# Attention, dense FFN and routed experts in one kernel: the join of split weight words, the 1e-9 of the softmax, and the order of the first tiles

## The chip, the cores and the metric

One core of a Trainium2 chip runs the whole program. The metric is the device time of one execution in microseconds; the time before is 1401.77 us, the median of three runs (1400.38 to 1402.29). The engines are called PE (TensorE), DVE (VectorE), ACT (ScalarE), POOL (GpSimd) and SP (SyncE, which issues most DMAs).

## The reference, cut to what matters

```python
# q, k, v: (8, 8, 576, 64) float32
k_p = k.reshape(B, H, Sp, 8, D).mean(axis=3)      # Sp = 72
v_p = v.reshape(B, H, Sp, 8, D).mean(axis=3)
scores = q @ k_p.T / 8;  scores -= scores.max(-1)
attn = exp(scores);  attn = attn / (attn.sum(-1) + 1e-9)
x = (attn @ v_p) as 4608 rows of 512
# dense FFN, w_in (512, 2048), w_out (2048, 512): 64-bit floats in DRAM
h = x @ w_in;  g = h if h >= 1, 0 if h <= -1, else (h + 1)**2 / 4
y = g @ w_out
# routed experts: each row goes to one of 8 experts by argmax(y @ w_gate)
out = softmax_weight * (relu(y @ w1[e]) @ w2[e])
```

The factors 64 and 8 of the means and the scale are folded into later constants.

## The kernel before, in words

The 4608 rows are 36 tiles of 128, in ten blocks of three, four or two tiles. Block 0 has tiles 0 to 2. For each block j the kernel runs 16 steps m: `f1(j, m)` multiplies the block's x by a 128-column piece of `w_in` into PSUM bank 0 or 1 (three products of a high and a low part, 12 matmuls), applies the activation, and `f2(j, m)` multiplies the result by a 128-row piece of `w_out` (nine matmuls in block 0). f1 runs two steps ahead (`AHEAD`). While block j runs, the attention of block j + 1 is done in its gaps: the deque `units` holds its pieces in order, and `slot(j, s)`, called twice a step, issues some. All order is written out by hand; an engine's queue is the order of the calls.

The activation of f1 is a relay. L600 on DVE clamps, L601 on ACT squares, then the closure `larger` issues L605 on DVE (the maximum) and L606 on ACT (the high part), and then the closure `lower` issues L264 on DVE (the low part), which also frees the PSUM bank for f1 two steps on. `larger` and `lower` stand in the deque `later`; `flush()` runs what stood in it when it was called, and what those closures append waits for the next flush. So in the first slot of a step `larger` runs, in the second `lower`.

Attention of a tile t: `u_qt` transposes q (L366, copy L368), `u_sc_all` computes the scores (L312), their maxima (L319) and differences (L321) on DVE, `exps` the exponential on ACT (L326), `rest` the row sums (L376), adds 1e-9 (L378), takes the reciprocal (L379), and lets POOL multiply (L390 or L382). `u_pt` brings the probabilities into transposed form (L412, copy L414; tiles 3 to 6 go through DVE transposes and DRAM instead), `u_pv` multiplies by the pooled values (L425) and writes x as a high part (L431, ACT) and a low part (L432, DVE). Keys are pooled by PE with an identity matrix (`u_kp`, L284), or with `pool_kv` by DVE (L249) or by POOL (L252 to L254), values by `pool_kv`.

The weights of the dense FFN come as 64-bit floats and are converted to 32 bits in block 0 alone: 32 conversions, 16 of `w_in` and 16 of `w_out`, in the order `order`, one for each call of `tick()`. A conversion i has three parts. `convert_a`: ACT copies the upper words, scaled (L527), and makes the sign words (L531). `convert_b` puts two word operations for DVE into the deque `pend`: the first (L539) joins the lowest bits and the sign in the PSUM bank `CV`, the second (L542) joins this with the scaled copy. `convert_c`, two ticks later, rounds to a high part on ACT (L549) and takes the low part on POOL (L264). `mix()` takes one element out of `pend`, the first of a conversion being empty; it is called at many places in the attention code, and `tick` begins with `mix(4)`. In block 0 a slot calls `tick` once while conversions last. The sign words have two buffers (`SGN`), the raw words six (`RB`), `CV` one.

The head, from L1106 on, does the attention of tiles 0 to 2 and the first conversions before f1(0, 0). Six conversions are copied in it (`CAHEAD + 1`), and one more with each of the first two calls of f1.

Of the kernel before, what the change touches and what calls it, by code (L numbers as in the profile page):

```python
# [13 lines left out]
ACTF = mybir.ActivationFunctionType  # L14
ALU = mybir.AluOpType
AX = mybir.AxisListType
# [8 lines left out]
def attention_ffn_routed_experts_kernel(  # L25
# [12 lines left out]
    nc = tc.nc  # L38
# [65 lines left out]
    def at(o, n, p=128):  # L104
        return AT[0:p, o:o + n]
# [1 line left out]
    def fx(o, n):  # L107
        return FX[:, o:o + n]

    KB = [at(576 * i, 4 * SP_).rearrange("p (a c) -> p a c", a=4) for i in range(2)]  # L110
    QB = [at(1152 + 512 * i, 512) for i in range(2)]
    QB2 = at(6336, 512)
    QT = at(2176, 512)
    SC = [at(2688, 576), at(7616, 576)]
    HEAD = blocks[0][1]
    RAW = [at(3264 + 512 * i, 512, SP_) for i in range(3)]
    KP = at(4800, 512, SP_)
    PAIR = [at(3264 + 1024 * i, 1024, SP_) for i in range(2)]
    YF = Y.rearrange("p t d -> p (t d)")
# [1 line left out]
          for a in [YF[:, 0:1024], YF[:, 1024:2048], at(5312, 1024)]  # L121
          + [WG.rearrange("p e d -> p (e d)")[:, 1024 * i:1024 * (i + 1)] for i in range(3)]]
    JK = at(7104, 512)
    PZ = at(1152, 768).rearrange("p (a h j) -> p a h j", a=3, j=32)
    PZ0 = at(6336, 768).rearrange("p (a h j) -> p a h j", a=3, j=32)
    PTB = PT.rearrange("p a (b x) -> p (a b) x", b=2)
    QR = at(5312, 2 * CHUNK * 128).rearrange("p (c u i) -> p c u i", c=4, i=32)
# [105 lines left out]
    def load_q(t):  # L233
        if t >= TURN0:
            return
        for p0, p1, b, s in segs(t):
            nc.sync.dma_start(
                out=qb_of(t)[p0:p1].rearrange("p (h d) -> p h d", h=H),
                in_=q[b, :, s:s + p1 - p0, :].rearrange("h s d -> s h d"))
# [19 lines left out]
    def bank():  # L259
        banks.rotate(-1)  # L260
        return banks[-1]
# [6 lines left out]
    def mix(n=1):  # L268
        for _ in range(min(n, len(pend))):
            pend.popleft()()  # L270
# [3 lines left out]
    def flush():  # L274
        for _ in range(len(later)):
            later.popleft()()

    def u_kp(b, c, raw):
# [6 lines left out]
                                 start=(r == 0), stop=(r == 7))  # L285
        nc.scalar.activation(out=KB[b][:, c], in_=pb[:, 0:SP_], func=ACTF.Copy)

    def u_kt_pair(b, c):

        pb = bank()  # L290
        nc.tensor.transpose(pb[:, 0:SP_], KP[:, c * 128:(c + 1) * 128], ident[0:SP_, 0:SP_])
        nc.scalar.activation(out=KB[b][:, c], in_=pb[:, 0:SP_], func=ACTF.Copy)

# [10 lines left out]
    def u_sc_all(t):  # L304
        pbs = [bank(), bank()]
        for c in range(4):
            for g in range(2):
                toks = slice(64 * g, 64 * g + 64)
                kb = KB[(t * 128 + 64 * g) // S % 2]
                for i in range(2):  # L310
                    rows = slice(64 * i, 64 * i + 64)
                    nc.tensor.matmul(pbs[i][toks, c * SP_:(c + 1) * SP_],  # L312
                                     qt_of(t)[rows, c * 128 + 64 * g:c * 128 + 64 * g + 64],
                                     kb[rows, c], start=True, stop=True)
        sc, sc3, smx = sc_of(t), sc3_of(t), smx3[:, t % 3]
        for i in range(2):
            src = pbs[i][:, 0:4 * SP_].rearrange("p (h c) -> p h c", h=4)
            hs = slice(i, H, 2)
            nc.vector.tensor_reduce(out=smx[:, hs], in_=src, axis=AX.X, op=ALU.max)  # L319
            mix()  # L320
            nc.vector.tensor_tensor(out=sc3[:, hs], in0=src,  # L321
                                    in1=smx[:, hs].to_broadcast([128, 4, SP_]), op=ALU.subtract)
        wide[0] = True

        def exps():
            nc.scalar.activation(out=sc, in_=sc, func=ACTF.Exp, scale=1.0 / 64)  # L326
            finish(t)
        if HEAD <= t < TURN0:
            later.append(exps)
        else:  # L330
            exps()
# [1 line left out]
    smx3 = sb.tile([128, 3, H, 1], F32, name="smx3")  # L333
    ssm3 = sb.tile([128, 3, H, 1], F32, name="ssm3")

    SCH = at(6848, 576)
    PTX = [WOF[2][0:SP_], WOF[3][0:SP_], PT[:, 0], PT[:, 1]]

    def qt_of(t):
        return FR if t == 1 else QT  # L340
# [1 line left out]
    def sc_of(t):  # L342
        return SCH if t == 2 else SC[t % 2]

    def sc3_of(t):
        return sc_of(t).rearrange("p (h c) -> p h c", h=H)

    def pt_of(t, hf):
        return PTX[(2 * t + hf) % 4] if t < HEAD else PT[:, hf]

    def u_qt(t):
        if t >= TURN0:
# [19 lines left out]
    def finish(t):  # L372
        sc3, ssm = sc3_of(t), ssm3[:, t % 3]

        def rest():
            nc.vector.tensor_reduce(out=ssm, in_=sc3, axis=AX.X, op=ALU.add)  # L376
            mix()
            nc.vector.tensor_scalar(ssm, ssm, 1e-9, None, op0=ALU.add)  # L378
            nc.vector.reciprocal(out=ssm, in_=ssm)  # L379
            if turned(t):  # L380
                eng = nc.vector if t >= TURN0 else nc.gpsimd
                eng.tensor_tensor(out=sc3, in0=sc3, op=ALU.mult,  # L382
                                  in1=ssm.to_broadcast([128, H, SP_]))
            elif t >= HEAD:
                later.append(norm)
            else:
                norm()

        def norm():
            nc.gpsimd.tensor_tensor(out=sc3, in0=sc3, in1=ssm.to_broadcast([128, H, SP_]),  # L390
                                    op=ALU.mult)
        later.append(rest)
# [59 lines left out]
    def load_pair(c):  # L452
        for i in range(2):
            load_kv(1, 2 * c + i, PAIR[c % 2][:, 512 * i:512 * (i + 1)])
# [63 lines left out]
    def cvt_dst(i):  # L518
        m, o = order[i]
        return (WOF[m % 4] if o else DFI[m % 3]), RB[i % NRB].rearrange(  # L520
            "p a (x w) -> p a x w", w=2)

    def convert_a(i):
        dst, rb = cvt_dst(i)

        high = rb[:, :, :, 1].bitcast(F32)
        nc.scalar.activation(out=dst.rearrange("p (a x) -> p a x", a=8), in_=high,  # L527
                             func=ACTF.Copy, scale=2.0 ** -112)

        sign = SGN[i % 2].bitcast(F16).rearrange("p (a x w) -> p a x w", a=8, w=2)  # L530
        nc.scalar.activation(out=sign[:, :, :, 1], in_=high, func=ACTF.Copy, scale=2.0 ** -60)  # L531

    def convert_b(i):

        dst, rb = cvt_dst(i)
        di, ci, sg = (x.bitcast(I32).rearrange("p (a x) -> p a x", a=8)
                      for x in (dst, CV, SGN[i % 2]))
        pend.append(lambda: None)
        pend.append(lambda: nc.vector.scalar_tensor_tensor(  # L539
            out=ci, in0=rb[:, :, :, 0], scalar=29, in1=sg, op0=ALU.logical_shift_right,  # L540
            op1=ALU.bitwise_or))
        pend.append(lambda: nc.vector.scalar_tensor_tensor(  # L542
            out=di, in0=di, scalar=3, in1=ci, op0=ALU.logical_shift_left, op1=ALU.bitwise_or))

    def convert_c(i):
        m, o = order[i]
# [25 lines left out]
    def tick():  # L572

        n = ticks[0]
        mix(4)
        if n > 0:
            more_raw(n - 1 + NRB)
        for f, i in ((convert_c, n - 2), (convert_a, n), (convert_b, n)):
            if 0 <= i < len(order) and order[i]:
                f(i)  # L580
        ticks[0] += 1

    def load_out(g):
# [522 lines left out]
    with tc.manual_schedule():  # L1106

        wgp = WG.rearrange("p e d -> p (e d)")[0:SP_]
        raw0 = [WG[0:SP_, i] for i in range(8)] + RAW + [
            FX[0:SP_, 512 * i:512 * (i + 1)] for i in range(1, 5)] + [PT[:, 0]]  # L1110
        hu = [tile_units(t) for t in range(HEAD)]

        def head_pool(i, eng):
            pool_kv(0, i, raw0[i], eng)

        def run_units(n):
            for _ in range(n):
                units.popleft()[1]()
            if qloads:
                qloads.popleft()()  # L1120

        load_q(0)
        for i in range(H):
            load_kv(0, i, raw0[i])
        load_q(1)
        load_q(2)
        for i in range(H, 2 * H):
            load_kv(0, i, raw0[i])
        for i in range(3):
            more_raw(i)  # L1130
        hu[0][0]()
        for c in range(2):
            u_kp(0, c, wgp[:, 1024 * c:1024 * (c + 1)])
        for i in (4, 5):
            head_pool(i, nc.vector)
        for i in (6, 7):
            head_pool(i, nc.gpsimd)
        nc.gpsimd.memset(WG[:, 6:8], 0.0)
        for i in range(3, NRB):
            more_raw(i)  # L1140
        hu[1][0]()
        for c in range(2, 4):
            u_kt_pair(0, c)
        for i in (8, 10, 12):
            head_pool(i, nc.gpsimd)
        hu[0][2]()
        hu[1][2]()
        hu[2][0]()
        head_pool(9, nc.vector)
        head_pool(14, nc.gpsimd)  # L1150
        flush()
        hu[2][2]()
        head_pool(15, nc.gpsimd)
        for i in (11, 13):
            head_pool(i, nc.vector)
        load_pair(0)
        load_pair(1)
        flush()
        tick()
        kv = deque([pair_step(c) for c in range(4)] + [kv_step(1, i) for i in range(H, 2 * H)])  # L1160
        line = [(0, 3), (0, 5), (1, 3), (0, 6), (1, 5), (2, 3), (1, 6), (2, 5), (2, 6)]
        for i, (t, n) in enumerate(line):
            hu[t][n]()
            flush()
            if i in (0, 2, 4, 6):
                tick()
        while ticks[0] < CAHEAD + 1:
            tick()
        banks.clear()
        banks.extend(ps[6:8])  # L1170

# [57 lines left out]
        for m in range(AHEAD):  # L1229
            f1(0, m)  # L1230
            flush()
            tick()
        for g, (j, m) in enumerate(steps):
            if m == 0:
                if j:
# [221 lines left out]
```

## Time and profile before

| what | value |
|---|---|
| median of three runs | 1401.77 us |
| the profiled execution, its own time | 1404.79 us |
| its span, from the first to the last instruction | 1402.8 us |
| busy in the span: PE, DVE, ACT, POOL | 97%, 55%, 31%, 26% |
| mean granted clock of TensorE | 0.993 |

Shares of busy time are means over stages with different limits: in a stretch PE may be full while the others idle, or DVE while PE waits. Durations of instructions that follow each other on one engine overlap a little, so the distance of two starts can be less than the duration of the first. In a timeline an entry in brackets is the idle time before an instruction and what ended it. Block 0 begins with the f1 at 38.11 us.

### The profile page before, as it was taken

How to read it: one execution, taken by the hardware profiler on the slowest of the kernel's cores; microseconds unless marked ns; L12 is line 12 of the kernel's file. 1: busy time of each engine (PE TensorE's matmuls, PEld its weight loads, DVE VectorE, ACT ScalarE, POOL GpSimd, SP SyncE). 2: the span in 40 equal slices, each digit the busy share in tenths (PEclk: the TensorE clock that was granted, in tenths of full speed). 3: DMA queues.
4: the chain of work that ended last, by engine and by line, in shares of the span. 5: the costliest groups of instructions: out<-in, count | busy, mean ns of one | idle time of the engine just before them, and what ended most of it. 6: DMA issues, size and time to landing. Idle time of an engine off the chain costs nothing. (4 is left out here: it accounts for less than half of the span.)

```text
span 1402.8 us, 22101 instructions
## 1 busy us (share of the span) xinstructions
PE 1357.5 (97%) x8082; PEld 1112.8 (79%) x8082; DVE 778.1 (55%) x1577; ACT 433.7 (31%) x729; POOL 358.7 (26%) x520
## 2 busy tenths in 40 slices
PE   6878999999999999999999999999999999999998
PEld 4767778878878778788788888888878888888786
DVE  5798556565666666575666556455532333323426
ACT  4567332222222222223222223343111111111335
POOL 5384736004304203413310011022221211111212
PEclk9999999999999999999999999999999999999999
DMA  9786647436636555545553344572543223331235
GB/s 254 226 261 240 182 136 214 129 122 194 164 124 187 153 149 168 171 155 143 165 157 111 98 152 130 192 263 72 195 129 106 91 74 113 99 111 61 79 127 187
DMA packets 170701, 213.45 MB, mean 152 GB/s; under 512 B 83432, under 2 KB 114440, under 8 KB 170569
## 3 DMA queue, kind: packets, MB, share of 16 engines
q1 hardware_dynamic: 135992, 102.29, 25.2%
q10 hardware_dynamic: 26784, 88.16, 18.8%
q0 software_dynamic: 7792, 21.35, 4.8%
q8 instruction: 69, 1.13, 0.3%
q14 instruction: 64, 0.52, 0.1%
HBM read 188.30 MB, written 47.03 MB: 168 GB/s over the span
## 5 line engine op out<-in xcount | busy, mean ns | idle before, releaser
L593 PE MATMUL ps<-XT,W 128*128 128x512 f32 (+2 forms) x640 | 243.8, 381 | 6.8 <-DVE FG L264 3.0
L595 PE MATMUL ps<-XT,W 128*128 128x512 f32 (+2 forms) x640 | 237.9, 372 | 2.7 <-POOL W L264 2.7
L594 PE MATMUL ps<-XT,W 128*128 128x512 f32 (+2 forms) x640 | 238.1, 372 | 0.2 <-DVE XT L432 0.2
L621 PE MATMUL ps<-WO,FG 128*128 128x512 f32 x576 | 231.6, 402 | 1.3 <-ACT FX L601 1.1
L622 PE MATMUL ps<-WO,FG 128*128 128x512 f32 x576 | 225.9, 392 | 0.0
L623 PE MATMUL ps<-WO,FG 128*128 128x512 f32 x576 | 225.2, 391 | 0.0
L601 ACT ACTIVATE FX<-FX,half 128x512 f32<-128x512 f32 (+2 forms) x152 | 104.0, 684 | 386.0 <-DVE FX L600 348.2
L600 DVE TENSOR_SCALAR FX<-ps 128x512 f32<-128x512 f32 (+2 forms) x152 | 96.7, 636 | 117.7 <-PE ps L595 116.9
L593 PEld LDWEIGHTS ps<-XT,W 128*128 128x128 f32 x640 | 121.8, 190 | 32.1 <-issue 3.4
L719 POOL DMA_INDIRECT perm_d<-idt,POSI x36 | 35.2, 978 | 417.6 <-DVE SM L705 353.0
L993 DVE SCALAR_TENSOR_TENSOR FG<-ps,FG 128x512 fp32r<-128x512 f32 (+1 forms) x64 | 43.2, 675 | 175.4 <-ACT FG L992 172.9
L595 PEld LDWEIGHTS ps<-XT,W 128*128 128x128 f32 x640 | 121.7, 190 | 22.3 <-POOL W L264 4.0
L605 DVE TENSOR_TENSOR ps<-FX,ps 128x512 f32<-128x512 f32 (+2 forms) x152 | 97.5, 641 | 72.8 <-ACT FX L601 71.4
L594 PEld LDWEIGHTS ps<-XT,W 128*128 128x128 f32 x640 | 121.7, 190 | 17.8 <-DVE XT L432 0.5
L621 PEld LDWEIGHTS ps<-WO,FG 128*128 128x128 f32 x576 | 108.5, 188 | 26.4 <-issue 3.0
L623 PEld LDWEIGHTS ps<-WO,FG 128*128 128x128 f32 x576 | 108.6, 188 | 23.7
L606 ACT ACTIVATE FG<-ps 128x512 fp32r<-128x512 f32 (+2 forms) x160 | 88.8, 555 | 123.9 <-DVE ps L605 112.2
L264 DVE TENSOR_TENSOR FG<-ps,FG 128x512 fp32r<-128x512 f32 (+2 forms) x160 | 100.8, 630 | 44.3 <-ACT FG L606 40.6
L622 PEld LDWEIGHTS ps<-WO,FG 128*128 128x128 f32 x576 | 108.7, 189 | 19.8
L252 POOL TENSOR_TENSOR AT<-AT 72x256 f32<-72x256 f32 x106 | 81.2, 766 | 136.3 <-DMA AT<-in_v_dram 68.7
L992 ACT ACTIVATE FG<-ps 128x512 fp32r<-128x512 f32 (+1 forms) x64 | 37.4, 584 | 244.8 <-PE ps L989 231.2
L987 PE MATMUL ps<-XT,W 128*128 128x512 f32 (+1 forms) x256 | 98.9, 386 | 2.9 <-ACT XT L971 2.5
(230 smaller groups left out, 2176.0 us busy)
## 6 DMA issues: line engine op xcount, KB each, us to landing
WO<-wo_d ACTq DMA_DIRECT2D x144, 512.0 KB
AT<-in_moe_w_dram SPq DMA_DIRECT2D x30, 1024.0 KB
p_d<-AT SPq DMA_DIRECT2D x29, 384.0 KB
AT<-in_v_dram SPq DMA_DIRECT2D x59, 144.0 KB
wo_d<-WO SPq DMA_DIRECT2D x16, 512.0 KB
AT<-in_k_dram SPq DMA_DIRECT2D x56, 144.0 KB
PT<-p_d SPq DMA_DIRECT2D x58, 128.0 KB
yrow_d<-Y ACTq DMA_DIRECT2D x7, 1032.0 KB
```

The lines of the kernel that those rows point to most:

```text
L264: eng.tensor_tensor(out=lo, in0=x, in1=r32(hi), op=ALU.subtract)
L593: nc.tensor.matmul(o, wi(m, 0, c), xh, start=(c == 0), stop=False)
L594: nc.tensor.matmul(o, wi(m, 0, c), xl, start=False, stop=False)
L595: nc.tensor.matmul(o, wi(m, 1, c), xh, start=False, stop=(c == KD - 1))
L600: nc.vector.tensor_scalar(r, o, -1.0, 1.0, op0=ALU.max, op1=ALU.min)
L601: nc.scalar.activation(out=r, in_=r, func=ACTF.Square, scale=0.5, bias=half)
L605: nc.vector.tensor_tensor(out=o, in0=r, in1=o, op=ALU.max)
L606: nc.scalar.activation(out=gh, in_=o, func=ACTF.Copy)
L621: nc.tensor.matmul(o, gh, WO[:, g % 4, 0], start=(m == 0), stop=False)
L622: nc.tensor.matmul(o, gh, WO[:, g % 4, 1], start=False, stop=False)
L623: nc.tensor.matmul(o, gl, WO[:, g % 4, 0], start=False, stop=(m == KF - 1))
L987: nc.tensor.matmul(o, e1(0)[:, c, ms], xh, start=(c == 0), stop=False)
```

## The change

- The scaled copy of the upper words (L527) goes into the PSUM bank `CV` and no longer into the target buffer. The first word operation shifts it in place and joins the sign words, the second joins the lowest bits, out of the raw words, and writes the target.
- The copies of a conversion (`convert_ab`) are put into `later` by `tick`, and run in the next flush.
- The scores of a tile have a 73rd column for each head, which is set to 1e-9 once; the row sum takes it in, and L378 falls away. Buffers move to make room.
- In the head, the exponentials of tiles 0 to 2 are called by hand, the memset of the sign words comes first, DVE pools three key heads, POOL one, and four value heads are summed by PE (`u_vp`: eight matmuls of 192 columns and eight of 64); before, `pool_kv` did all eight, three of them on DVE and five on POOL, and now POOL does the other four. Tiles 0, 1 and 2 are finished one after the other; their probabilities have six buffers.
- Four conversions are copied before f1(0, 0) where it was six. Three more ticks follow f1(0, 0), one f1(0, 1).

The diff, cut to what the steps touch (moved buffers mostly left out):

```diff
@@ -285,6 +287,19 @@
+    def u_vp(more):
+        pb = bank()
+        n = len(RAW)
+        raw = at(RAW0, n * 512, SP_).rearrange("p (h r d) -> p h r d", h=n, r=8)
+        for x, h0, h1 in ((raw, 0, n), (more.rearrange("p (h r d) -> p h r d", h=1, r=8), n, n + 1)):
+            dst = pb[0:SP_, h0 * D:h1 * D].rearrange("p (h d) -> p h d", h=h1 - h0)
+            for r in range(8):
+                nc.tensor.matmul(dst, ident[0:SP_, 0:SP_], x[:, :, r], start=(r == 0),
+                                 stop=(r == 7))
+        nc.scalar.activation(out=VS[:, 0, 0:(n + 1) * D], in_=pb[0:SP_, 0:(n + 1) * D],
+                             func=ACTF.Copy)
     def u_kt_pair(b, c):
@@ -323,9 +338,9 @@
         def exps():
-            nc.scalar.activation(out=sc, in_=sc, func=ACTF.Exp, scale=1.0 / 64)
+            nc.scalar.activation(out=sc3, in_=sc3, func=ACTF.Exp, scale=1.0 / 64)
             finish(t)
-        if HEAD <= t < TURN0:
+        if t < TURN0:
             later.append(exps)
@@ -333,8 +348,8 @@
-    SCH = at(6848, 576)
-    PTX = [WOF[2][0:SP_], WOF[3][0:SP_], PT[:, 0], PT[:, 1]]
+    SCH = at(6848, SCW)
+    PTX = [VS[:, 1], FR[0:SP_], PT[:, 0], PT[:, 1], WOF[2][0:SP_], WOF[3][0:SP_]]
@@ -342,11 +357,14 @@
+    def sc4_of(t):
+        return sc_of(t).rearrange("p (h c) -> p h c", h=H)
     def sc3_of(t):
-        return sc_of(t).rearrange("p (h c) -> p h c", h=H)
+        return sc4_of(t)[:, :, 0:SP_]
     def pt_of(t, hf):
-        return PTX[(2 * t + hf) % 4] if t < HEAD else PT[:, hf]
+        return PTX[2 * t + hf] if t < HEAD else PT[:, hf]
@@ -373,9 +391,9 @@
         def rest():
-            nc.vector.tensor_reduce(out=ssm, in_=sc3, axis=AX.X, op=ALU.add)
-            mix()
-            nc.vector.tensor_scalar(ssm, ssm, 1e-9, None, op0=ALU.add)
+            nc.vector.tensor_reduce(out=ssm, in_=sc4_of(t), axis=AX.X, op=ALU.add)
+            if t >= HEAD:
+                mix()
             nc.vector.reciprocal(out=ssm, in_=ssm)
@@ -521,10 +539,10 @@
     def convert_a(i):
-        dst, rb = cvt_dst(i)
+        _, rb = cvt_dst(i)
         high = rb[:, :, :, 1].bitcast(F32)
-        nc.scalar.activation(out=dst.rearrange("p (a x) -> p a x", a=8), in_=high,
+        nc.scalar.activation(out=CV.rearrange("p (a x) -> p a x", a=8), in_=high,
                              func=ACTF.Copy, scale=2.0 ** -112)
@@ -537,10 +555,15 @@
         pend.append(lambda: nc.vector.scalar_tensor_tensor(
-            out=ci, in0=rb[:, :, :, 0], scalar=29, in1=sg, op0=ALU.logical_shift_right,
+            out=ci, in0=ci, scalar=3, in1=sg, op0=ALU.logical_shift_left, op1=ALU.bitwise_or))
+        pend.append(lambda: nc.vector.scalar_tensor_tensor(
+            out=di, in0=rb[:, :, :, 0], scalar=29, in1=ci, op0=ALU.logical_shift_right,
             op1=ALU.bitwise_or))
-        pend.append(lambda: nc.vector.scalar_tensor_tensor(
-            out=di, in0=di, scalar=3, in1=ci, op0=ALU.logical_shift_left, op1=ALU.bitwise_or))
+    def convert_ab(i):
+        mix(len(pend))
+        convert_a(i)
+        convert_b(i)
@@ -575,9 +598,10 @@
             more_raw(n - 1 + NRB)
-        for f, i in ((convert_c, n - 2), (convert_a, n), (convert_b, n)):
-            if 0 <= i < len(order) and order[i]:
-                f(i)
+        if 0 <= n - 2 < len(order) and n != 3:
+            convert_c(n - 2)
+        if n < len(order):
+            later.append(lambda: convert_ab(n))
         ticks[0] += 1
@@ -1106,7 +1130,7 @@
         wgp = WG.rearrange("p e d -> p (e d)")[0:SP_]
-        raw0 = [WG[0:SP_, i] for i in range(8)] + RAW + [
+        raw0 = [WG[0:SP_, i] for i in range(6)] + [VS[:, 1], PT[:, 1]] + RAW + [
             FX[0:SP_, 512 * i:512 * (i + 1)] for i in range(1, 5)] + [PT[:, 0]]
@@ -1119,53 +1143,66 @@
+        nc.gpsimd.memset(WG[:, 6:8], 0.0)
+        for t in range(3):
+            nc.gpsimd.memset(sc4_of(t)[:, :, SP_:SP_ + 1], 1e-9)
         load_q(0)
...
         load_q(2)
-        for i in range(H, 2 * H):
+        for i in (12, 13, 8, 9, 10, 11, 14, 15):
             load_kv(0, i, raw0[i])
...
             u_kp(0, c, wgp[:, 1024 * c:1024 * (c + 1)])
-        for i in (4, 5):
+        for i in (4, 5, 6):
             head_pool(i, nc.vector)
-        for i in (6, 7):
-            head_pool(i, nc.gpsimd)
-        nc.gpsimd.memset(WG[:, 6:8], 0.0)
+        head_pool(7, nc.gpsimd)
         for i in range(3, NRB):
...
             u_kt_pair(0, c)
-        for i in (8, 10, 12):
+        for i in (12, 13, 14):
             head_pool(i, nc.gpsimd)
         hu[0][2]()
+        hu[2][0]()
+        later.popleft()()
         hu[1][2]()
-        hu[2][0]()
-        head_pool(9, nc.vector)
-        head_pool(14, nc.gpsimd)
+        rest = later.popleft()
+        later.popleft()()
+        rest()
+        head_pool(15, nc.gpsimd)
+        later.popleft()()
+        hu[2][2]()
+        exps2 = later.popleft()
+        tick()
         flush()
-        hu[2][2]()
-        head_pool(15, nc.gpsimd)
-        for i in (11, 13):
-            head_pool(i, nc.vector)
+        u_vp(raw0[11])
+        exps2()
         load_pair(0)
         load_pair(1)
+        hu[0][3]()
+        flush()
+        hu[0][5]()
+        hu[0][6]()
+        tick()
+        flush()
+        hu[1][3]()
+        hu[1][5]()
+        hu[1][6]()
+        tick()
+        hu[2][3]()
+        hu[2][5]()
+        convert_c(1)
+        hu[2][6]()
         flush()
         tick()
+        flush()
         kv = deque([pair_step(c) for c in range(4)] + [kv_step(1, i) for i in range(H, 2 * H)])
-        line = [(0, 3), (0, 5), (1, 3), (0, 6), (1, 5), (2, 3), (1, 6), (2, 5), (2, 6)]
-        for i, (t, n) in enumerate(line):
-            hu[t][n]()
-            flush()
-            if i in (0, 2, 4, 6):
-                tick()
-        while ticks[0] < CAHEAD + 1:
-            tick()
         banks.clear()
@@ -1229,7 +1266,9 @@
             flush()
-            tick()
+            while ticks[0] < CAHEAD + 2 + m:
+                tick()
+                flush()
         for g, (j, m) in enumerate(steps):
...
                 if j:
```

## Rows read from the trace of the kernel before

**Rows 1.** Stretches: us, busy PE, PEld, DVE, ACT, POOL (count), granted clock, DMA, GB/s.

```profile
68.00:141.10 73.10, 59.89 (x431) 48.69 (x430) 67.59 (x110) 50.95 (x90) 46.56 (x51) 0.93 0.75 250
...
124.70:141.10 16.40, 15.91 (x106) 13.56 (x107) 13.39 (x26) 10.83 (x19) 8.04 (x9) 0.81 0.44 160
...
200.00:400.00 200.00, 200.00 (x1277) 161.01 (x1274) 126.22 (x253) 57.15 (x93) 52.31 (x97) 1.00 0.55 159
```

**Rows 2.** The same view, of line 539 alone: DVE busy time and instructions.

```profile
68.00:141.10 73.10, 21.11 (x20) 0.93 0.75 250
```

**Rows 3.** The same view, of line 378 alone.

```profile
68.00:141.10 73.10, 4.54 (x4) 0.93 0.75 250
```

**Rows 4.** Timeline of DVE in block 0: start, duration (us), line, shapes.

```profile
42.31 0.56 DVE L600 TENSOR_SCALAR FX<-ps 128x384 f32<-128x384 f32 x1 [1.81 <-PE ps L595]
...
68.06 0.56 DVE L600 TENSOR_SCALAR FX<-ps 128x384 f32<-128x384 f32 x1 [1.72 <-PE ps L595]
...
105.29 1.42 DVE L539 SCALAR_TENSOR_TENSOR ps<-WG 128x512 int32<-128x512 int32 x1
106.82 0.69 DVE L542 SCALAR_TENSOR_TENSOR FX<-FX,ps 128x512 int32<-128x512 int32 x1
...
108.66 0.55 DVE L605 TENSOR_TENSOR ps<-AT,ps 128x384 f32<-128x384 f32 x1
109.12 0.69 DVE L539 SCALAR_TENSOR_TENSOR ps<-WG 128x512 int32<-128x512 int32 x1
109.84 0.69 DVE L542 SCALAR_TENSOR_TENSOR FX<-FX,ps 128x512 int32<-128x512 int32 x1
110.45 0.55 DVE L264 TENSOR_TENSOR FG<-ps,FG 128x384 fp32r<-128x384 f32 x1
110.92 0.55 DVE L600 TENSOR_SCALAR FX<-ps 128x384 f32<-128x384 f32 x1
...
141.07 0.51 DVE L600 TENSOR_SCALAR FX<-ps 128x384 f32<-128x384 f32 x1
```

**Rows 5.** Timeline of ACT beside those.

```profile
109.24 0.49 ACT L606 ACTIVATE FG<-ps 128x384 fp32r<-128x384 f32 x1 [1.23 <-DVE ps L605]
109.63 0.62 ACT L549 ACTIVATE W<-FX 128x512 fp32r<-128x512 f32 x1
110.15 0.67 ACT L527 ACTIVATE FX<-WG 128x512 f32<-128x512 f32 x1
110.71 0.80 ACT L531 ACTIVATE WG<-WG 128x512 f16<-128x512 f32 x1
```

**Rows 6.** Timeline of the head and the first steps, several engines.

```profile
8.13 1.98 DVE L249 TENSOR_REDUCE AT<-WG 72x64 f32<-72x512 f32 x2 [6.89 <-DMA WG<-in_k_dram]
...
12.78 0.95 POOL L1138 MEMSET WG<- 128x1024 f32 x1
...
13.09 1.24 PE L312 MATMUL ps<-AT 64*64 64x72 f32 x32
...
15.22 1.11 PE L366 MATMUL ps<-ident,AT 128*128 128x128 f32 x4
...
21.38 2.77 PE L412 MATMUL ps<-ident,AT 128*72 128x128 f32 x12 [0.99 <-POOL AT L390]
...
27.57 1.12 PE L425 MATMUL ps<-FX,VS 72*64 72x128 f32 x8 [0.53 <-ACT FX L414]
...
38.11 0.69 PE L593 MATMUL ps<-XT,W 128*128 128x384 f32 x1 [1.42 <-DVE XT L432]
...
48.62 0.60 PE L366 MATMUL ps<-ident,AT 128*128 128x128 f32 x4
...
56.05 0.69 PE L593 MATMUL ps<-XT,W 128*128 128x384 f32 x1
```

More of the change, by code (lines that the diff above doesn't have):

```diff
@@ L108, in fx @@
         return FX[:, o:o + n]
-    KB = [at(576 * i, 4 * SP_).rearrange("p (a c) -> p a c", a=4) for i in range(2)]
-    QB = [at(1152 + 512 * i, 512) for i in range(2)]
+    KB = [at(288 * i, 4 * SP_).rearrange("p (a c) -> p a c", a=4) for i in range(2)]
+    QB = [at(1160 + 512 * i, 512) for i in range(2)]
     QB2 = at(6336, 512)
-    QT = at(2176, 512)
-    SC = [at(2688, 576), at(7616, 576)]
+    QT = at(7616, 512)
+    SCW = H * (SP_ + 1)
+    SC = [at(2184, SCW), at(576, SCW)]
     HEAD = blocks[0][1]
-    RAW = [at(3264 + 512 * i, 512, SP_) for i in range(3)]
+    RAW0 = 3264
+    RAW = [at(RAW0 + 512 * i, 512, SP_) for i in range(3)]
     KP = at(4800, 512, SP_)
@@ L123, in attention_ffn_routed_experts_kernel @@
     JK = at(7104, 512)
-    PZ = at(1152, 768).rearrange("p (a h j) -> p a h j", a=3, j=32)
+    PZ = at(1160, 768).rearrange("p (a h j) -> p a h j", a=3, j=32)
     PZ0 = at(6336, 768).rearrange("p (a h j) -> p a h j", a=3, j=32)
@@ L314, in u_sc_all @@
                                      kb[rows, c], start=True, stop=True)
-        sc, sc3, smx = sc_of(t), sc3_of(t), smx3[:, t % 3]
+        sc3, smx = sc3_of(t), smx3[:, t % 3]
         for i in range(2):
```

## The prediction

> **What bounds the kernel now.** I read the stages first [rows 1]. From 149 us on TensorE (PE) is busy for 200.0 of 200 us in the stretch shown, so nothing that VectorE (DVE) or ScalarE (ACT) saves there can shorten the run. Between 68 and 141 us, most of block 0, DVE is the full engine: 67.6 of 73.1 us, and PE has gaps. The reader is to see that only the head (to 38.1 us) and block 0 can give time, and that every microsecond by which block 0 ends later or earlier is carried to the end unchanged, since PE is full behind it.
>
> Then why DVE is full. The first word operation of a conversion (L539) took 21.1 us in that stretch for 20 instructions [rows 2]; the undisturbed ones take 0.69 us [rows 4], so 20 x 0.69 = 13.8 us would do and 7.3 us are waits inside the instruction. The tiny addition of 1e-9 (L378, eight elements a row) took 4.5 us in four instructions [rows 3]. The second word operation (L542), which has one operand in PSUM, is 0.69 us also where the first had just taken 1.42 [rows 4]; L539 has both in SBUF. DVE stands still in only 5.5 of the 73.1 us.
>
> **The change, part by part.**
>
> *Word operations.* Each keeps two DVE instructions of 0.69 us, but none has two SBUF operands any more. Gain in that stretch: 7.3 us. The page "SBUF — State Buffer" of the Trainium skill (section "SBUF: two separate sides") says that a DVE operation with two SBUF inputs and a GpSimd operation lock each other out for a whole instruction; the 1.42 us instruction [rows 4] agrees. *The 73rd summand* removes L378: 4.5 us more. The reduction reads 73 instead of 72 elements a head, and the exponential eight strips instead of one; nothing there is on a path. In the later blocks the same removal is worth nothing, as PE covers it.
>
> *The copy into the PSUM bank.* This is the part that costs. Today ACT's two copies of a conversion (L527, L531) write buffers that are free early, and are issued ahead of the step's L606. After the change L527 writes the one bank CV, so it must wait for the second word operation of the conversion before; and the copies are put into the list of late work behind the step's `larger`, so ACT does L606 first. Behind both stands the next first word operation, which opens the next slot on DVE, ahead of that slot's scores and of L264. So DVE finishes L605, and then waits: 0.03 us until L606 starts, 0.39 until the next ACT instruction, 0.56 from L527 to L531, 0.80 for L531, 0.03 back [rows 4, 5]: 1.8 us in each step with two conversions, and nothing on DVE's queue may pass. In the other slot the copies (0.03 + 0.56 + 0.80 + 0.03 = 1.42 us after L542's end) run beside L264 and L600, which fill 0.94 us (110.53 to 111.47): 0.5 us of wait, in the seven of ten steps in which no row sum stands there.
>
> The sum from 68.06 to 141.07, ten steps: DVE busy 67.6 - 7.3 - 4.5 = 55.8; new waits 10 x 1.8 + 7 x 0.5 = 21.5; together 77.3 against 73.1. Of the 5.5 us that DVE waits today (PE results, key copies) I leave 1 us in: **+5.1 us**. Bounds: all 5.5 us stay (+9.7), or half of the waits find other DVE work (-6.5). The copy into PSUM has no row; nearest are L606, 0.49 us for 384 columns out of PSUM, and L549, 0.62 us between SBUF buffers for 512 [rows 5]; I take today's pace, as the input doesn't change. The page "ScalarE: Activation LUTs" of the Trainium skill (section "Step-by-step: what each stage is for") calls PSUM the quicker target for ACT, without a figure; no row here shows it, and 0.1 us less a copy would by estimate take 2 us off these 20 conversions.
>
> *The head.* It is a chain through all engines. The memset of the sign buffers leaves its place in POOL's queue, at 12.78 us, and goes to the start, where POOL is idle; three 128x8 memsets join it there at no more than the 0.95 us of the big one [rows 6], hidden until DVE sums the first key head at 8.13, behind its load [rows 6]. Key head 6 goes to DVE, so the first scores start some 0.8 us earlier (12.3 for 13.1). The loads of V change order only, eight as before; SP's queue is no longer. The value sums by PE are 16 matmuls of 8 x 192 + 8 x 64 = 2048 columns; at the pace of the twelve transposes (2.77 us for 1536) 3.7 us [rows 6]. They stand where PE waited for the first probabilities anyway, and take two chains of additions off POOL and three value sums off DVE: first transposes at 20.8 instead of 21.4. But then ACT's copies of conversion 1 wait for conversion 0's second word operation, which stands behind tile 0's L432: ACT idles from 23.4 to 27.4, and tile 1's two copies of 0.6 us stand behind it. I get PV of tile 0 finished at 25.4, 3.3 us earlier (28.7 today, 27.57 + 1.12), and the first matmul of f1 at 37.5 against 38.1 [rows 6]. Bounds: 1.5 us later, to 4 us earlier if PE runs this part at full speed. It does not today: four transposes take 1.11 us at 15.2 and 0.60 at 48.6 [rows 6], so this is the lower of the two levels, although the granted-clock column shows 1.00 there.
>
> *The first steps.* Where before has six conversions copied when f1 begins, after has four; the rest is issued between f1(0) and f1(1) on DVE and ACT. Each turn of the single bank costs 0.03 + 0.56 + 0.80 + 0.03 on ACT and 0.72 + 0.69 on DVE: 2.85 us. From 37.5: clamp of f1(0) at 41.7 (4.2 behind, as today), its L264 done 45.3, conversions 4 and 5 until 50.5, only then the clamp of f1(1); its square stands behind conversion 6's copies (52.4), its L264 ends at 54.8. f1(2) follows, conversion 8 ends at 60.9, then the scores of tile 3 (1.7 us); the key sums of PE need their bank, and f1(3) starts at 62.9 against 56.05 [rows 6]. The clamp of f1(4) comes at 73.7 against 68.06 [rows 4]: **+5.6 us**, with the head in it. Bounds: -1 (the queue of conversions catches up beside PE) to +9.
>
> *Sum:* 5.6 + 5.1 = +10.7. The profiled execution took 1404.79 us (span 1402.8, 2.0 around it), and stands 3.0 above the median of 1401.77. 1404.8 + 10.7 = 1415.5; taken to the median **1412.5 us**.
>
> **The rivals.**
>
> *The lock waits decide and the copies fit in.* If DVE's new waits are filled, the gain of 11.8 us (7.3 + 4.5) stays and only the first steps are paid: -11.8 + 5.6 = -6.2, 1395.6 us. It turns when the wait per step falls under 1.2 us (11.8 over ten steps). For it: the lock waits are in the rows beyond doubt. Against it: both copies lie between L605 and the next word operation in program order. The locking rule of the Trainium skill's page "SBUF — State Buffer" would by itself give this time.
>
> *PE reaches its higher level in the head*, through the denser matmuls: 4 us off the head, 1408.5. Against it: the transposes and PV of the head today stay at the lower one.
>
> *PE falls to its lower level more often in block 0*, because it waits more; [rows 1] has 0.81 granted from 124.7 to 141.1, where PE was busy. A step's 12 + 9 matmuls would double beyond DVE's 7.7 us a step: some 6 us more, 1418.5.
>
> *The join does not avoid the wait*: the first word operation still reads one operand from SBUF. Then 7.3 us come on top, 1419.8. L542 with the same kinds of operand never shows it.
>
> *Nothing measurable*: the first steps catch up and the middle gains as it loses, 1402.
>
> **How the numbers follow.** Forecast 0.47, lock waits 0.20, higher level 0.10, lower level 0.12, nothing 0.08, join 0.03. About 0.2% (2.8 us) is what a measurement here can tell from no change. Faster 0.20, same 0.08, slower 0.72. The forecast's own range is 1406 to 1418. The whole range goes from 1392, which takes in most of the lock rival with its bounds, to 1420.
>
> **What would show it.** Right: in block 0 L539's successor at 0.69 us each; DVE idle about 1.8 us a step ahead of it, with ACT's sign copy as releaser; f1(0) near 37.5, f1(3) past 60; the clamp of f1(14) near 152 instead of 141.07; PE from there as before. Wrong: DVE still without gaps in block 0, or f1(4)'s clamp before 68, or f1(0) before 35; then the copies ran ahead, or the head gained more than I give it.

## The result and the profile after

The changed kernel took 1414.14 us, the median of four runs (1412.04 to 1415.08), beside 1402.03 us for the kernel before in the same comparison: ratio 1.0087, 95% interval 1.0069 to 1.0104. It is slower by 12.1 us. The forecast was 1412.5, and slower was its likeliest side. The execution shown here took 1412.04 us (span 1410.2), the lowest of the four; the profiled execution of before (1404.79) stood 2.8 above its median. Between two single traces I read nothing under some 2 us: a second profiled execution of before reached the clamp of f1(14) 0.9 us earlier than the first, and took 1401.86.

Lines have moved: the clamp L600 is now L624, the maximum L605 is L629, L606 is L630, L264 is L266, the scaled copy L527 is L545, the sign copy L531 is L549, and the word operations L539 and L542 are L557 and L559.

First the stretches, with the columns of [rows 1], and then the stretch of block 0 that ends with the clamp of f1(14), whose counterpart in before is 68.06 to 141.07:

```profile
68.00:141.10 73.10, 57.81 (x444) 48.23 (x444) 51.13 (x93) 47.91 (x88) 39.56 (x47) 0.91 0.79 255
...
200.00:400.00 200.00, 200.00 (x1252) 161.00 (x1254) 127.89 (x252) 56.95 (x92) 58.28 (x109) 1.00 0.55 161
...
71.60:150.85 79.25, 60.81 (x431) 49.78 (x430) 57.04 (x106) 51.60 (x92) 42.45 (x51) 0.91 0.73 237
```

PE is full behind block 0, as before. In block 0 DVE is no longer the full engine: 51.1 of 73.1 us where [rows 1] has 67.6. It has 22 us without work in the 79.25 us of the last line. The first word operation alone, in the view of [rows 2]:

```profile
68.00:141.10 73.10, 13.26 (x19) 0.91 0.79 255
```

That is 0.70 us each, where [rows 2] has 1.06. The waits inside the instruction are gone. The clamps of f1(0), f1(4) and f1(14), which answer to 42.31, 68.06 and 141.07 in [rows 4]:

```profile
37.76 0.56 DVE L624 TENSOR_SCALAR FX<-ps 128x384 f32<-128x384 f32 x1 [1.50 <-PE ps L619]
...
71.60 0.56 DVE L624 TENSOR_SCALAR FX<-ps 128x384 f32<-128x384 f32 x1 [0.33 <-PE ps L619]
...
150.85 0.51 DVE L624 TENSOR_SCALAR FX<-ps 128x384 f32<-128x384 f32 x1
```

So block 0's relay starts 4.6 us earlier, is 3.5 late at f1(4) and 9.8 late at f1(14). Where it is lost is in the waits of DVE by line and releaser, 40 to 165 us (total, times, longest). In before the wait for the sign copy came once:

```profile
DVE ps L539 <- ACT WG L531: 0.4, 1, 0.4
```

In the changed kernel:

```profile
DVE ps L557 <- ACT WG L549: 26.7, 20, 1.8
DVE AT L624 <- PE ps L619: 5.1, 1, 5.1
DVE FX L624 <- PE ps L619: 2.7, 3, 1.3
```

One step of it, first DVE, then ACT (start, duration, line, in brackets the idle time before and what ended it):

```profile
90.26 0.55 DVE L629 TENSOR_TENSOR ps<-FX,ps 128x384 f32<-128x384 f32 x1
92.61 0.70 DVE L557 SCALAR_TENSOR_TENSOR ps<-ps,WG 128x512 int32<-128x512 int32 x1 [1.80 <-ACT WG L549]
93.34 0.69 DVE L559 SCALAR_TENSOR_TENSOR FX<-WG,ps 128x512 int32<-128x512 int32 x1
93.95 0.55 DVE L266 TENSOR_TENSOR FG<-ps,FG 128x384 fp32r<-128x384 f32 x1
94.42 0.55 DVE L624 TENSOR_SCALAR AT<-ps 128x384 f32<-128x384 f32 x1
95.45 0.70 DVE L557 SCALAR_TENSOR_TENSOR ps<-ps,WG 128x512 int32<-128x512 int32 x1 [0.49 <-ACT WG L549]
```

```profile
90.84 0.49 ACT L630 ACTIVATE FG<-ps 128x384 fp32r<-128x384 f32 x1 [1.23 <-DVE ps L629]
91.23 0.64 ACT L545 ACTIVATE ps<-WG 128x512 f32<-128x512 f32 x1
91.81 0.77 ACT L549 ACTIVATE WG<-WG 128x512 f16<-128x512 f32 x1
...
94.07 0.63 ACT L545 ACTIVATE ps<-WG 128x512 f32<-128x512 f32 x1 [1.02 <-DVE FX L559]
94.63 0.79 ACT L549 ACTIVATE WG<-WG 128x512 f16<-128x512 f32 x1
```

After the maximum (L629) DVE stands still while ACT does the high part (L630) and both copies, one after the other, and the low part (L266) and the next clamp stand behind the word operations. In the second slot of the step the copy waits for L559 (94.07), and DVE another 0.49 us. Between 71.60 and 150.85 us there are ten waits of 1.76 to 1.83 us and five of about half a microsecond, 20.3 us together.

The head, PE's queue:

```profile
16.39 2.85 PE L298 MATMUL ps<-AT,ident 72*72 72x192 f32 x16
19.07 1.19 PE L298 MATMUL ps<-FX,ident 72*72 72x64 f32 x16
20.10 1.04 PE L430 MATMUL ps<-ident,AT 128*72 128x128 f32 x8
...
27.21 1.98 PE L443 MATMUL ps<-PT,VS 72*64 72x128 f32 x16 [2.82 <-ACT PT L432]
29.12 1.92 PE L430 MATMUL ps<-ident,AT 128*72 128x128 f32 x8
...
33.64 0.69 PE L617 MATMUL ps<-XT,W 128*128 128x384 f32 x1 [0.70 <-ACT XT L449]
```

The first f1 starts at 33.64 us, 4.5 earlier than in [rows 6]. The value sums of L298 take 3.9 us, and the eight transposes right behind them 1.04 us (0.13 each, where the twelve in [rows 6] took 0.23 each). After a wait of 2.82 us for the copies of conversion 1 and tile 1 on ACT, eight transposes take 1.92 us again. The granted clock says the same, PE alone in two stretches (1.00 is 2.4 GHz, 0.50 is 1.2):

```profile
20.00:24.00 4.00, 2.89 (x35) 1.00 1.09 399
...
27.00:30.00 3.00, 2.79 (x21) 0.50 0.86 213
```

In before that column is 1.00 over the slow transposes too, so in the head the durations are the rows to read.

### The profile page after: what moved, and what is told of

Read it like the earlier page. It is cut to its first block, busy times and chain, and to the rows that moved or that the text cites. A ratio compares the mean times of both kernels' runs of the same rounds, so it can differ in the third digit from the quotient of the medians.

```text
span 1410.2 us, 22130 instructions
## 1 busy us (share of the span) xinstructions
PE 1360.1 (96%) x8114; PEld 1116.9 (79%) x8114; DVE 755.6 (54%) x1539; ACT 435.5 (31%) x730; POOL 350.2 (25%) x517
## 5 line engine op out<-in xcount | busy, mean ns | idle before, releaser
L624 DVE TENSOR_SCALAR FX<-ps 128x512 f32<-128x512 f32 (+2 forms) x152 | 96.9, 638 | 122.3 <-PE ps L619 121.9
L617 PEld LDWEIGHTS ps<-XT,W 128*128 128x128 f32 x640 | 121.7, 190 | 37.5 <-ACT W L572 10.4
L629 DVE TENSOR_TENSOR ps<-FX,ps 128x512 f32<-128x512 f32 (+2 forms) x152 | 97.5, 641 | 72.8 <-ACT FX L625 72.8
L630 ACT ACTIVATE FG<-ps 128x512 fp32r<-128x512 f32 (+2 forms) x160 | 88.8, 555 | 129.4 <-DVE ps L629 120.8
L266 DVE TENSOR_TENSOR FG<-ps,FG 128x512 fp32r<-128x512 f32 (+2 forms) x160 | 100.7, 630 | 44.2 <-ACT FG L630 42.8
L254 POOL TENSOR_TENSOR AT<-AT 72x256 f32<-72x256 f32 x104 | 76.9, 740 | 133.8 <-DMA AT<-in_v_dram 71.4
```

The lines of the kernel that those rows point to most:

```text
L266: eng.tensor_tensor(out=lo, in0=x, in1=r32(hi), op=ALU.subtract)
L617: nc.tensor.matmul(o, wi(m, 0, c), xh, start=(c == 0), stop=False)
L624: nc.vector.tensor_scalar(r, o, -1.0, 1.0, op0=ALU.max, op1=ALU.min)
L629: nc.vector.tensor_tensor(out=o, in0=r, in1=o, op=ALU.max)
L630: nc.scalar.activation(out=gh, in_=o, func=ACTF.Copy)
```

## The experiments

Three things might cost the time: the single bank (a copy waits for the word operations of the conversion before it), the late place of the copies (behind the step's `larger`), and the head with its four conversions instead of six ahead of f1. The **order theory** puts the loss on the late place; the **bank theory**, its rival, on the bank alone. The head was kept in the first three experiments, and the two other parts were undone singly and together. All were timed with repetitions beside the kernel before. Differences between two experiments are differences of medians; where the two were timed at different times, the ratios to before can put them about 1 us elsewhere.

**The join as before, copies still late.**

```diff
-        nc.scalar.activation(out=CV.rearrange("p (a x) -> p a x", a=8), in_=high,
+        nc.scalar.activation(out=dst.rearrange("p (a x) -> p a x", a=8), in_=high,
...
-            out=ci, in0=ci, scalar=3, in1=sg, op0=ALU.logical_shift_left, op1=ALU.bitwise_or))
+            out=ci, in0=rb[:, :, :, 0], scalar=29, in1=sg, op0=ALU.logical_shift_right,
+            op1=ALU.bitwise_or))
         pend.append(lambda: nc.vector.scalar_tensor_tensor(
-            out=di, in0=rb[:, :, :, 0], scalar=29, in1=ci, op0=ALU.logical_shift_right,
-            op1=ALU.bitwise_or))
+            out=di, in0=di, scalar=3, in1=ci, op0=ALU.logical_shift_left, op1=ALU.bitwise_or))
```

> The changed kernel with the word join as before (scaled copy to the target in SBUF, first word operation with two SBUF operands); the copies still stand in the list of late work. Order theory (DVE waits because ACT's copies stand behind L606 of the relay): the wait of DVE ahead of the first word operation stays near 1.8 us in each step, the lock waits come back partly on top; 1410 to 1418 us. Bank theory (DVE waits because the one PSUM bank makes each copy wait for the conversion before): the waits vanish, 1396 to 1403 us.

Measured: 1409.23 us, ratio 1.0041 (1.0023 to 1.0058). Its waits of DVE, same view, and the clamps of f1(4) and f1(14):

```profile
DVE ps L557 <- ACT WG L549: 22.4, 14, 1.8
```

```profile
69.19 0.56 DVE L624 TENSOR_SCALAR FX<-ps 128x384 f32<-128x384 f32 x1 [0.58 <-PE ps L619]
...
148.34 0.51 DVE L624 TENSOR_SCALAR FX<-ps 128x384 f32<-128x384 f32 x1
```

The waits of 1.8 us are there without any bank, and the ten steps take 79.15 us, as in the changed kernel. But f1(4) is 2.4 us earlier, and the time lies just under the order theory's range.

**The join in the bank, copies early.** From conversion 8 on they are called at once instead of being put into the list:

```diff
-            later.append(lambda: convert_ab(n))
+            if n < 8:
+                later.append(lambda: convert_ab(n))
+            else:
+                convert_ab(n)
```

> The changed kernel, but in the slots of block 0 (ticks from 8 on) the copies are issued by the tick itself, ahead of the relay's L606, as before; the bank stays. Order theory: DVE's waits of 1.8 us shrink to 0.9 or less, those of 0.5 stay; 9 to 13 us less than the changed kernel, 1400 to 1405 us. Bank theory: the waits stay as long as they are, 1411 to 1417 us.

Measured: 1407.33 us, ratio 1.0028 (1.0016 to 1.0039), between the two theories.

```profile
DVE ps L557 <- ACT WG L549: 9.8, 17, 1.4
```

```profile
71.92 0.56 DVE L627 TENSOR_SCALAR FX<-ps 128x384 f32<-128x384 f32 x1 [2.93 <-PE ps L622]
...
143.48 0.51 DVE L627 TENSOR_SCALAR FX<-ps 128x384 f32<-128x384 f32 x1
```

Ten steps in 71.56 us: the late place was the cost there. But f1(4) is as late as in the changed kernel: the first steps are the bank's cost. (The first eight conversions keep their late copies in this run and in the next.)

**Both undone.** Both diffs above together; the head, its four conversions and the 73rd summand stay.

> Both undone together: join as before and copies issued by the tick from tick 8 on; the changed head, its four conversions and the 73rd summand stay. Both theories: no new wait, the lock waits of 7.3 us are back, the 4.5 us of L378 stay away; 1393 to 1399 us. If it is the head and the first steps of the change that cost: 1403 us or more.

Measured: 1399.49 us, ratio 0.9978 (0.9965 to 0.9990): faster than before, half a microsecond above what was expected.

```profile
68.56 0.56 DVE L627 TENSOR_SCALAR FX<-ps 128x384 f32<-128x384 f32 x1 [3.06 <-PE ps L622]
...
137.91 0.51 DVE L627 TENSOR_SCALAR FX<-ps 128x384 f32<-128x384 f32 x1
...
68.56:137.91 69.35, 20.88 (x20) 0.95 0.80 260
```

The last line is L557 alone. It waits inside the instruction as in [rows 2] (20.88 us for 20), and yet these ten steps, 69.35 us, are shorter than those with the bank, 71.56. For two single traces that is a small difference, but three more with the old join and early copies, further below, have 68.8 to 69.7 us. So from 1399.5 us the late copies cost 9.7, the bank 7.8, and both together 14.6: neither theory holds alone. Each is a wait for the other engine, and where both are there the waits partly fall together.

**The kernel before without the addition of 1e-9**, with nothing in its place:

```diff
-            nc.vector.tensor_scalar(ssm, ssm, 1e-9, None, op0=ALU.add)
```

> The kernel before without line 378: the addition of 1e-9 to the row sums is left out (a row sum is at least 1, since its maximum is in it). If DVE bounds block 0, the 4.5 us that it took from 68 to 141 us come off: 1396 to 1399 us. If other work hides it: 1401 to 1403 us.

Measured: 1402.64 beside 1402.52 us, ratio 1.0002 (0.9993 to 1.0012). The 4.5 us of [rows 3] on the engine that was 92% busy are worth less than 1 us, by the lower end of the interval. Its trace (the clamp is L599 here) has f1(14) earlier all the same, by 3.0 and 2.1 us beside the two traces of before, and its ten steps take 70.28 us:

```profile
138.03 0.51 DVE L599 TENSOR_SCALAR FX<-ps 128x384 f32<-128x384 f32 x1
```

That execution took 1400.58 us, 2.1 under its median; I go by the ten timed ones.

**Both undone, and the value heads 0 to 3 pooled by POOL and DVE again.**

```diff
-        u_vp(raw0[11])
         exps2()
+        for i in (8, 10):
+            head_pool(i, nc.gpsimd)
+        for i in (9, 11):
+            head_pool(i, nc.vector)
```

> The kernel of e3_old_join_early_copies (1399.5 us), but value heads 0 to 3 are pooled as before, two by POOL and two by DVE, and not by PE. Clock theory (the value sums bring PE to its higher level in the head, and the early f1 is worth its 4.5 us): first f1 back near 38 us, 1402 to 1405 us. Queue theory (the early start is used up by the conversions queued behind f1(0)): first f1 later, but the clamp of f1(4) within 1.5 us of 68.6, 1398 to 1401 us.

Measured: 1404.63 us, ratio 1.0022 (1.0011 to 1.0034), 5.1 us more than with both undone (6.2 by the two ratios). PE in its head:

```profile
20.54 1.92 PE L430 MATMUL ps<-ident,AT 128*72 128x128 f32 x8 [4.00 <-POOL AT L408]
25.35 0.70 PE L443 MATMUL ps<-VS 72*64 72x128 f32 x4 [2.90 <-POOL VS L256]
...
38.01 0.69 PE L620 MATMUL ps<-XT,W 128*128 128x384 f32 x1 [1.42 <-DVE XT L450]
```

Without the value sums the transposes take 1.92 us from the start, and f1 begins at 38.01 us where before has 38.11. The head's gain is the value sums' doing, and it is carried on: the clamp of f1(4) comes at 72.57 us instead of 68.56, so the queue theory, which had it within 1.5 us of 68.6, is out. How much of it is PE's pace and how much the wait for POOL's pooling (2.90 us) stays open, since this edit brings back both.

**Both undone, and six conversions copied ahead of f1(0) instead of four.**

```diff
-        tick()
-        flush()
+        for _ in range(3):
+            tick()
+            flush()
```

> The kernel of e3_old_join_early_copies, but with two more ticks ahead of f1(0, 0), six conversions as in the kernel before. Queue theory: the work is the same and only stands elsewhere; clamp of f1(0) about 3 us later, that of f1(4) within 1 us of 68.6, 1398 to 1401 us. Clock theory: each microsecond by which f1 begins later is lost, 1402 us or more.

Measured: **1394.76 us** (eight runs), ratio 0.9950 (0.9935 to 0.9965): the fastest of all, under both theories. DVE from the end of the head, first with four, then with six:

```profile
35.28 0.69 DVE L560 SCALAR_TENSOR_TENSOR FX<-FX,ps 128x512 int32<-128x512 int32 x1
37.99 0.56 DVE L627 TENSOR_SCALAR FX<-ps 128x384 f32<-128x384 f32 x1 [2.02 <-PE ps L622]
...
45.18 0.55 DVE L627 TENSOR_SCALAR AT<-ps 128x384 f32<-128x384 f32 x1
```

```profile
36.67 0.69 DVE L560 SCALAR_TENSOR_TENSOR FX<-FX,ps 128x512 int32<-128x512 int32 x1
37.27 0.55 DVE L627 TENSOR_SCALAR FX<-ps 128x384 f32<-128x384 f32 x1
...
40.78 0.55 DVE L627 TENSOR_SCALAR AT<-ps 128x384 f32<-128x384 f32 x1
...
62.93 0.56 DVE L627 TENSOR_SCALAR FX<-ps 128x384 f32<-128x384 f32 x1 [3.74 <-PE ps L622]
...
131.75 0.50 DVE L627 TENSOR_SCALAR FX<-ps 128x384 f32<-128x384 f32 x1
```

With four, DVE waits 2.02 us for f1(0), and three conversions then stand between its clamp and that of f1(1): 7.2 us from one to the other. With six, DVE does word operations while PE multiplies, and the second clamp follows 3.5 us behind the first. The clamp of f1(4) comes 5.6 us earlier, and the ten steps behind it take 68.8 us, no different. Of these 5.6 us, 3.6 lie between the first f1 and that clamp; the other 2.0 are there because f1 began at 31.36 instead of 33.34. The work ahead of f1 on PE is the same in both, and PE kept its quicker pace longer here. With seven ahead, below, f1 began at 31.03, so whether this is chance stays open.

**The changed kernel with six copied ahead of f1(0)**, the same edit on it:

```diff
-        tick()
-        flush()
+        for _ in range(3):
+            tick()
+            flush()
```

> The changed kernel with two more ticks ahead of f1(0, 0), and nothing else altered: bank and late copies stay. In e6 the same two ticks took 4.7 us off, because DVE's word operations filled its wait for f1(0). If the three costs (two conversions behind f1(0), the place of the copies, the bank) stand side by side: 1407 to 1410 us, with DVE's waits of 1.8 us unaltered. If the bank makes these conversions wait for each other wherever they stand: 1411 to 1415 us.

Measured: 1413.71 us, ratio 1.0073 (1.0056 to 1.0091), as the changed kernel. The first clamp waits now, and f1(4) is where it was:

```profile
42.48 0.55 DVE L624 TENSOR_SCALAR FX<-ps 128x384 f32<-128x384 f32 x1
...
71.50 0.56 DVE L624 TENSOR_SCALAR FX<-ps 128x384 f32<-128x384 f32 x1 [0.55 <-PE ps L619]
```

With one bank the conversions follow each other at its pace wherever they stand. So the 4.7 us that two more conversions ahead of f1 are worth (1399.5 to 1394.8; 3.9 by the two ratios) are there only with the old join.

**Both undone, and seven copied ahead of f1(0)**, against the kernel with six:

```diff
-        for _ in range(3):
+        for _ in range(4):
             tick()
             flush()
```

> The kernel of e3_old_join_early_copies with three more ticks ahead of f1(0, 0), seven conversions. DVE's wait for f1(0) is filled already by six (clamp of f1(0) at 37.3, 2 us behind the end of its matmuls): the seventh only delays that clamp by the 1.4 us of its word operations; 1394 to 1397 us. If more conversions in front always gain: 1390 to 1393 us.

Measured: 1398.66 us, ratio 0.9972 (0.9960 to 0.9984): 3.9 more than with six, and above both ranges that were expected. Its clamp of f1(0) comes at 38.68 and that of f1(1) at 40.38, but f1(4) at 63.07, no earlier than with six, and PE now waits 5.0 us for low parts (twice) where it waited 2.0. Its ten steps and the rest are hardly told apart from those with six in the traces (69.66 us, f1(14) at 132.73). Where all of the 3.9 us lie stays open.

The two kernels were also profiled once more, side by side:

> The kernel before, unchanged, profiled a second time, to see how far block 0 differs between two executions: clamp of f1(4) and f1(14) within 3 us of 68.06 and 141.07.

> The changed kernel, unchanged, profiled a second time: waits of DVE for the sign copies again 26 to 27 us in 20 instructions, since their length is set by program order alone; clamp of f1(14) within 3 us of 150.85.

They took 1401.86 and 1412.29 us, with the clamps of f1(14) at 140.16 and 151.25. The waits for the sign copy are the same row to the digit (26.7 us, 20 times, 1.8 at most). From that clamp to the end of the execution it is 1260.5 to 1265.4 us in all twelve traces of this case, worked out as the execution's time less the clamp's start: what happens in block 0 is carried to the end, within 2.5 us. Behind that clamp the changed kernel is no slower (1261.2 and 1261.0 us, where before has 1263.7 and 1261.7).

## Why the prediction was right, step by step

**The side, the size and the place were right.** 1412.5 was forecast and 1414.1 measured. Block 0 decides, PE is full behind it, and the loss is DVE waiting for ACT's copies. That the number came so close is in part luck: two misses cancelled, as shown next, and the traces place 9.8 us at the clamp of f1(14) (11.1 in the second pair) where the medians are 12.1 apart. The rest is no more than single executions differ by.

**The ten steps.** The forecast was DVE busy 55.8 us, waits of 21.5 us (ten of 1.8, seven of 0.5) and +5.1 us. Measured from 71.60 to 150.85: busy 57.0, waits 20.3 (ten of 1.8, five of 0.5), 79.25 us for 73.01, +6.2. The 1 us that the forecast left of today's other waits was 1.9. (Two of its sums are slightly off: 77.3 and 1 less 73.1 is 5.2, not 5.1, and the parts of a bank turn add up to 2.83, not 2.85. Neither matters.) Of the rivals, a lower clock in block 0 had no part that shows: granted were 0.91 in [rows 1]'s stretch, where before has 0.93, and PE was busy for 60.8 us of these ten steps, 1.0 more than in before. The relay L605, L606, L527, L531, back to DVE could be worked out from the rows of before because only its order changed, not its parts.

**The first steps and the head.** The step that failed in size is the head: "the first matmul of f1 at 37.5" was 33.64, near the bound of 4 us earlier, and "f1(0) before 35" was one of the prediction's own signs of being wrong. ACT's copy of conversion 1, which was to start at 27.4, started at 25.41. The rival of a higher level in the head came true in part, as the transposes at 20.10 show. From there the count of bank turns held as far as the clamp of f1(1), 12.9 us from the first f1 (13.0 forecast); to that of f1(4) it was 38.0 (36.2 forecast). f1(3) started at 59.96, a hair short of the "past 60" that was to show the forecast right. So f1(4) came +3.5 us late instead of +5.6: 3.9 less by the head, 1.8 more by the steps behind it. The two misses, -2.1 in the first steps and +1.1 in the ten steps, partly cancel. Beside before the head's gain is used up at once: f1(0) is clamped 4.6 us earlier, f1(1) 1.2 later (46.53 for 45.35), because its clamp stands behind the conversions that before had copied ahead. That an early start is not lost as such shows with the old join: there the run without value sums on PE, with f1 at 38.01, was 5.1 us slower.

**The word operations.** "None has two SBUF operands any more" held: no first word operation of the ten steps took over 0.70 us. The page "SBUF — State Buffer" of the Trainium skill (section "SBUF: two separate sides") has an operation with two SBUF inputs lock against GpSimd; the rows agree, and the rival that the join does not avoid the wait is out.

**Where the reasoning was wrong though the sum was right.** "If DVE's new waits are filled, the gain of 11.8 us (7.3 + 4.5) stays" is the step that failed; it stands in a rival, and the forecast's sum credits the same 11.8 us. It took DVE's busy time for the bound of the ten steps. With the bank and early copies the waits for sign copies there are 5.3 us, about half a microsecond a step and well under the 1.2 at which that rival was to turn; DVE is busy 56.6 of 71.56 us, and 1.4 us of the 11.8 are won (0.5 beside the second trace of before, whose ten steps took 72.05). With the old join DVE is busy 63.0, and the steps take 69.35. The two stretches, the second to within 0.05 us:

```profile
71.92:143.48 71.56, 58.30 (x429) 48.04 (x427) 56.64 (x106) 50.88 (x89) 41.19 (x50) 0.95 0.81 257
...
68.60:137.90 69.30, 56.97 (x425) 47.07 (x424) 63.04 (x105) 49.61 (x89) 45.23 (x50) 0.95 0.80 260
```

So 6.4 us less of DVE work did not make the ten steps shorter. The kernel without line 378 gains nothing that its timed runs can tell. Here a full engine that feeds a relay was no bound that could be bought down one for one. Why the ten steps with the old join are some 3 us shorter than in before, with the lock waits back, was not taken apart: line 378 is gone there, and what stands ahead of them has changed. What comes next is in these rows, the waits of PE between the clamps of f1(4) and f1(14) in the kernel with the bank and early copies:

```profile
PE ps L443 <- DMA PT<-p_d: 7.4, 3, 3.2
PE ps L384 <- DVE AT L336: 2.3, 3, 1.3
PE ps L620 <- ACT W L572: 1.8, 2, 1.0
```

The way of the probabilities through DRAM ends PE's longest waits (6.2 us in three waits in before). In the changed kernel the sum held because its waits lie in DVE's own queue, where nothing can pass, and there they add up. Which wait sets the 69 to 72 us with early copies was not settled. Nor was the join tried with a second bank, since block 0 has none free, nor the lock wait removed without the bank.

## What to carry to other kernels

Before a wait inside an instruction is traded for a wait between engines, write down the relay that the new wait makes, instruction by instruction in queue order: a copy put behind another engine's step costs its whole chain each time, and one shared buffer in place of a target for each makes conversions follow each other at that buffer's pace, also those that were to be done in advance. Busy time taken off the fullest engine counts only until something else is the last to be ready; take one such piece out alone first and see whether the run moves. When a head gets faster, check that what stands behind it is ready: here two more conversions ahead of f1 were worth 4.7 us with the old join, and nothing that could be measured with one bank.

## What the runs showed of the hardware

TensorE ran the head's transposes at 0.13 us each right behind 3.9 us of unbroken value sums, and at 0.24 again after it had waited 2.8 us. No rule follows: with both parts undone the transposes at 24.46 us were at 0.24 after waits of 0.83 and 0.81 us. The copy of 128x512 into PSUM took 0.62 to 0.65 us, hardly under the 0.65 to 0.69 into SBUF between 40 and 150 us of before; the page "ScalarE: Activation LUTs" of the Trainium skill (section "Step-by-step: what each stage is for") calls PSUM the quicker target, and here that is 0.03 us on average. The 0.1 us that the prediction tried out is not there. The lock waits depend on when POOL works. Between the clamps of f1(4) and f1(14) in before, nine of the 20 first word operations took over 1 us, and each of them began while POOL was at a two-input operation; the other eleven, which began without one, ahead of one or in its last 0.15 us, took 0.68 to 0.70. POOL under the 1.42 us instruction of [rows 4], which began at 105.29:

```profile
104.86 1.29 POOL L264 TENSOR_TENSOR W<-FX,W 128x512 fp32r<-128x512 f32 x1
```

With the old join and late copies, 20 first word operations took 16.28 us between the two clamps, with early copies 20.88, and nothing about the operands differs between the two.
